# Attention with a gated MLP mixer on one core: score tiles in two 2-bank and three 1-bank PSUM buffers, half of the 64-shifts on GpSimd, conversions ahead of shifts, and a new first and last step

## The chip, the cores and the metric

The kernel runs on one core of one Trainium2 chip. The metric is the device time of one execution in microseconds (us), smaller is better. A core has these engines: TensorE (PE in the profile; PEld is its weight load), VectorE (DVE), ScalarE (ACT), GpSimd (POOL) and SyncE (SP, which here only issues DMAs). SBUF is the on-chip memory; PSUM, of which this kernel fills eight banks of 128 x 512 fp32 (seven for scores and projections, one for the accumulator), is where TensorE leaves its results.

## The reference, cut to what matters

```python
# x: 1 x 2048 x 512, 32 heads of 16 dimensions
g = sigmoid((x * gate_w).sum(-1, keepdims=True))
qkv = (x @ wqkv) ...                       # q, k, v by heads
scores = einsum("bhqd,bhkd->bhqk", q, k) * (16 ** -0.5)
a = einsum("bhqk,bhkd->bhqd", softmax(scores), v) ... @ wo
b = <layernorm, w1, gelu, shifts along S, w2, residual, layernorm, w3, gelu, w4, residual>
return g * a + (1 - g) * b
```

The costly part is the softmax: 32 heads x 2048 x 2048 scores are 2048 tiles of 128 x 512 exponentials.

## The kernel before

The tiles are worked off in 32 rounds of 64. TensorE computes transposed scores into PSUM. Each tile's exponential is then done by one of two engines.

ScalarE takes groups of three or two tiles at a time with one `activation`:

```python
WIDTHS, RING = (3, 2), 2          # psA buffers of 3 and 2 banks for ScalarE; 2 single banks for the rest
NPA, NPD, NW = 6, 16, 9
...
job = act(hold, ops, lambda: nc.scalar.activation(out=pb.slot[:, 0:n], in_=buf.slot[:, 0:n], func=ACT.Exp,
                                                  scale=0.25), acq=[pb], frees=[buf], prio=3)
```

VectorE builds its exponentials out of bits. A conversion ("p1") turns a score tile from a single PSUM bank into uint16 numbers that, read as bf16, are a rough exponential. For each pair of tiles these numbers are then shifted by 32, 64 and 96, and all four patterns are multiplied by V, so that their average is a good exponential. A VectorE tile therefore costs TensorE four P·V matmuls where a ScalarE tile costs one. The shifts by 32 and 64 are VectorE's, the third is GpSimd's:

```python
        def p1():
            nc.vector.tensor_scalar(out=pr["buf"].slot[:, h * 512:(h + 1) * 512], in0=buf.slot[:], scalar1=BITS_MUL,
                                    scalar2=BITS_ADD, op0=ALU.mult, op1=ALU.add)
        j1 = dve(598, [o], p1, acq=[pr["buf"]] if h == 0 else [], frees=[buf], prio=2, name="p1")
    # ... cut ...
        for k in range(1, 4):
            def sh(k=k):
                d = [b.slot for b in bufs]
                if k < 3:
                    nc.vector.tensor_scalar(out=d[k][:, 0:w], in0=d[0][:, 0:w], scalar1=float(SHIFT * k), scalar2=None,
                                            op0=ALU.add)
                else:
                    nc.gpsimd.tensor_scalar(out=d[k][:, 0:w], in0=d[2][:, 0:w], scalar1=1.0, scalar2=float(SHIFT),
                                            op0=ALU.mult, op1=ALU.add)
            if k < 3:
                j = dve(0.26 * w + 72.0, pr["jobs"], sh, prio=1, acq=[bufs[k]], frees=[bufs[0]])
            else:
                j = gp(0.833 * w + 165.0, last, sh, prio=1, acq=[bufs[k]], frees=[bufs[2]])
```

Which tile goes to which engine, and in what order each engine issues its instructions, is fixed when the program is built. The kernel has its own planner, a small event model of the engines (`class Sim`): the first number in `act(...)`, `dve(...)` and `gp(...)` is how long the planner believes the instruction holds its engine in ns, and the ready job with the lowest `prio` goes first. A pair's shift, 1024 elements wide, is planned at 0.26 x 1024 + 72 = 338 ns on VectorE and 0.833 x 1024 + 165 = 1018 ns on GpSimd. **The planner treats the engines as independent.**

At the end of each round the accumulator is copied, its denominators are gathered, inverted and spread by DMAs, GpSimd multiplies (`oT`), and DMAs pack the product into `oD` buffers for the output projection.

The softmax here doesn't subtract the row's maximum and nothing guards it: scores larger than these inputs give would overflow.

Of the kernel before, what the change touches and what calls it, by code (L numbers as in the profile page):

```python
# [75 lines left out]
class Gen:  # L76


    def __init__(self, units, deps, at, name, acq="ring"):
        self.units, self.deps, self.at, self.name = units, deps, at, name  # L80
        self.pos = 0
        self.buf = Buf(acq, 1)
        self.ops = [o for u in units for o in u]
        self.gone = False
# [144 lines left out]
def kernel(  # L229
# [27 lines left out]
    WIDTHS, RING = (3, 2), 2  # L257

    NPA, NPD, NW = 6, 16, 9
# [8 lines left out]
    def slots(name, n, shape, dt=BF16, where=const):  # L268
# [10 lines left out]
    zero = const.tile([P, 512], BF16, name="zero")  # L279
    mE = const.tile([P, 1], F32, name="mE")  # L280
# [18 lines left out]

    sim = Sim({  # L300
        **{f"psA{w}{n}": slots(f"psA{n}", 1, [P, 512 * w], F32, ps) for n, w in enumerate(WIDTHS)},
        "ring": slots("ring", RING, [P, 512], F32, ps),
        "PA": slots("PA", NPA, [P, 1536]),
# [50 lines left out]
    for c0, c1 in ((0, 128), (128, 512)):  # L354
        nc.scalar.dma_start(out=W("k")[:, :, c0:c1], in_=wrows(A_wqkv[:, D + c0:D + c1]))
        nc.scalar.dma_start(out=wq[:, :, c0:c1], in_=wrows(A_wqkv[:, c0:c1]))
    nc.scalar.dma_start(out=W("v")[:], in_=wrows(A_wqkv[:, 2 * D:3 * D]))
    nc.scalar.dma_start(out=gw[:], in_=gate_w.rearrange("(kt p) -> p kt", p=P))
    dl_w["k0"] = sim.add(Job("SP", 1, 6000.0, [], None))
    dl_w["k"] = sim.add(Job("SP", 1, 12000.0, [], None))  # L360
    dl_w["v"] = sim.add(Job("SP", 1, 14000.0, [], None))
# [6 lines left out]
    for c in range(NCH):  # L368
        for k in range(KT):
            j_xT[c, 0, k] = load_xT(c, k, 0, 2600.0 + 1150.0 * (4 * c + k + 1), 0)  # L370
    for c in range(NCH):
        j_x.append(dma(22000.0 + 2000.0 * c, [], lambda c=c: nc.sync.dma_start(
            out=x_sb[:, 4 * c:4 * c + 4, :], in_=x_flat[c * 512:(c + 1) * 512, :].rearrange("(t p) d -> p t d", p=P)),
            prio=1))
# [13 lines left out]

    gp(150, [], lambda: nc.gpsimd.memset(mhalf[:], -0.5), prio=0)
    j_io = gp(200, [], lambda: nc.gpsimd.iota(mi[:], pattern=[[0, 1]], base=0, channel_multiplier=1), prio=0)  # L390
    j_z = dve(300, [], lambda: nc.vector.memset(zero[:], 0.0), prio=0)
    j_m1 = dve(100, [j_io], lambda: nc.vector.tensor_scalar(out=mb[:], in0=mi[:], scalar1=16, scalar2=None,
# [11 lines left out]
    def gen(name, at, deps, mms, N=512, M=P):  # L404

        get = lambda: g.buf.slot
        units = []
        for i, (lf, rf) in enumerate(mms):
            st, sp = i == 0, i == len(mms) - 1
            if COL and M == P:  # L410
                units.append([Op("col", j, lambda j=j, lf=lf, rf=rf, st=st, sp=sp: nc.tensor.matmul(  # L411
                    get()[32 * j:32 * j + 32, 0:N], lhsT=lf(32 * j, 32 * j + 32), rhs=rf(), start=st, stop=sp,
                    tile_position=(0, 32 * j), skip_group_check=True), ns=N * 0.42, name=name) for j in range(4)])
            else:
                units.append([Op("full", None, lambda lf=lf, rf=rf, st=st, sp=sp: nc.tensor.matmul(
                    get()[0:M, 0:N], lhsT=lf(0, M), rhs=rf(), start=st, stop=sp), ns=N * 0.42, name=name)])
        g = Gen(units, deps, at, name)
        gens.append(g)
        return g
# [8 lines left out]

    j_k = {}

    def k_proj(G, c, at):
# [3 lines left out]
        g.ops[-1].frees += [wb["k"], wb[f"x{c}0"]]  # L435
        j_k[G, c] = evac(g, PSUM_NS, lambda ps: nc.vector.tensor_copy(out=kT[G][:, c * 512:(c + 1) * 512], in_=ps[:]),
# [5 lines left out]
    def q_proj(G, c, at):  # L442
# [3 lines left out]
                  lambda k=k: W(f"x{c}{part}")[:, k, :]) for k in range(KT)])  # L446
# [21 lines left out]
    def v_proj(t, at):  # L468
        c = t // 4
        g = gen("v", at, [j_xT[c, 0, k] for k in range(KT)] + [dl_w["v"]],  # L470
                [(lambda a, b, k=k: W(f"x{c}0")[:, k, (t % 4) * P + a:(t % 4) * P + b],
                  lambda k=k: W("v")[:, k, :]) for k in range(KT)])
        g.ops[-1].frees += [wb["v"], wb[f"x{c}0"]]
        j_v[t] = evac(g, PSUM_NS, lambda ps: nc.vector.tensor_copy(
            out=V0[:, t, :, 1:DH + 1], in_=ps[:].rearrange("p (h d) -> p h d", h=H)), prio=2)
        j_v[t].deps.append(j_v1)
        if t % 2 == 0:
            j_v2[t] = gp(750, [j_v[t]], lambda: nc.gpsimd.tensor_scalar(
                out=V2[:, t // 2], in0=V0[:, t], scalar1=W2, scalar2=1.0, op0=ALU.mult, op1=ALU.mult), prio=1)


    def gate(at):
        g = gen("z", at, [j_xT[c, 0, k] for c in range(NCH) for k in range(KT)], [], M=P)
# [97 lines left out]
    j_o2 = {}  # L581

    def mlp2(c, s2, at_of, jgate):
        last = normalise(c, 1, [s2[t] for t in range(4 * c, 4 * c + 4)], 0)
        jx1g = {}
        for t in range(4 * c, 4 * c + 4):
# [15 lines left out]
        for t in range(4 * c, 4 * c + 4):  # L602
# [13 lines left out]
            else:  # L616
                j_o2[t] = evac(g, PSUM_NS, lambda ps, t=t: nc.vector.scalar_tensor_tensor(
                    out=x_sb[:, t, :], in0=ps[:], scalar=omg[:, t:t + 1], in1=x_sb[:, t, :], op0=ALU.mult,
                    op1=ALU.add))
                sim.jobs["DVE"][-1].deps.append(jx1g[t])  # L620

    def mix(g, t, deps):
        ob = Buf("ot", 1)
# [265 lines left out]
    for t in range(NT):  # L889
        v_proj(t, max(0, 3 * t - 2))  # L890
# [197 lines left out]
```

## Time and profile before

Three executions took 891.75 to 893.7 us, median 893.31.

| | before |
|---|---|
| median time | 893.3 us |
| tiles done by ScalarE / by VectorE | 1534 / 514 |
| ScalarE busy in the long stretches | 94% |
| first exponential starts | 12.6 us |
| longest wait of ScalarE in mid run | 14.6 us |
| last exponential ends, to the end | 24 us |

First the page of the kernel before: busy time of each engine with its share of the span, three of the rows that show the span in 40 slices (each digit is a busy share in tenths), and the chain of work that ended last, by engine.

```profile
PE 786.6 (89%) x8981; PEld 251.1 (28%) x8982; DVE 693.1 (78%) x1361; ACT 755.7 (85%) x631; POOL 390.5 (44%) x400
...
DVE  4774988798899998877875787678878568887871
ACT  3364999899998999998993998999998889999990
POOL 2243764444467793434432444234444234344440
...
PE 48%; ACT 23%; DVE 12%; issue 7%; DMA 4%; POOL 4%; SPq 2%; POOLq 0%; ACTq 0%; DVEq 0%
```

After the first four slices ScalarE sits at 8s and 9s, with a dip to 3 in slice 22; VectorE and GpSimd have room. The chain runs mostly through PE and ScalarE.

Next the same page's costliest groups: line, engine, operation, output from input, shapes and count; then total busy us and mean ns of one; then the engine's idle time before them and who ended most of it.

```profile
L741 ACT ACTIVATE PA<-psA 128x1536 bf16<-128x1536 f32 x614 | 709.7, 1259 | 97.8 <-PE acc L821 38.4
L793 POOL TENSOR_SCALAR PD<-PD 128x1024 uint16<-128x1024 uint16 x257 | 269.8, 1050 | 432.4 <-DVE PD L790 310.4
L766 DVE TENSOR_SCALAR PD<-ring 128x512 uint16<-128x512 f32 x514 | 340.7, 682 | 106.6 <-PE ring L665 90.1
...
L790 DVE TENSOR_SCALAR PD<-PD 128x1024 uint16<-128x1024 uint16 x514 | 219.5, 464 | 6.3 <-PE acc L821 0.7
```

The four kinds of work in question: exponentials (L741), GpSimd's shift (L793), VectorE's conversions from PSUM (L766) and VectorE's shifts (L790). The shifts' mean of 464 ns hides a wide spread, as all the instructions of that one line show (minimum, median, maximum in ns):

```profile
L790 DVE TENSOR_SCALAR PD<-PD x514: 359/419/1501, 14.1 to 861.8; 128x1024 uint16<-128x1024 uint16 x172
```

Half of the shifts take 419 ns or less.

Last, the windows view of the kernel before: start and end of the stretch, its length, and busy us of PE, PEld, DVE, ACT and POOL (instructions in brackets), then TensorE's clock, DMA share and GB/s.

```profile
0.00:100.00 100.00, 79.14 (x858) 25.68 (x858) 64.26 (x133) 53.14 (x47) 38.80 (x52) 0.91 0.41 97
100.00:470.00 370.00, 332.22 (x3751) 105.20 (x3754) 319.79 (x632) 346.21 (x292) 192.83 (x196) 0.97 0.17 45
470.00:490.00 20.00, 16.16 (x239) 6.38 (x235) 10.16 (x18) 4.99 (x6) 6.00 (x6) 1.00 0.09 28
490.00:865.00 375.00, 352.51 (x4134) 111.82 (x4123) 294.72 (x574) 351.35 (x291) 151.60 (x147) 0.95 0.08 22
865.00:889.00 24.00, 6.62 (x16) 2.04 (x16) 4.12 (x7) 0.00 (x0) 1.26 (x1) 0.63 0.12 37
```

ScalarE is busy 346.21 of 370 us and 351.35 of 375, 94% in both. The other three rows are the head, a stall and the tail.

### The profile page before, as it was taken

The page shows a single profiled execution, that of the slowest core. Times are in us where ns is not written, and L with a number is a line of the kernel's source. Part 1 is how long each engine was busy: PE and PEld are TensorE (multiplying, and loading weights), DVE is VectorE, ACT ScalarE, POOL GpSimd, SP SyncE. Part 2 cuts the span into 40 slices and gives each one's busy share as a digit, 9 for nine tenths or more (in the row PEclk, how much of TensorE's full clock was granted, in tenths as well). Part 3 has the DMA queues.
Part 4 walks back from the last instruction along what each step waited for, and adds up shares of the span by engine and source line. Part 5 has one row for each costly group of instructions (what it writes and reads, how often), then busy time and mean ns, then how long its engine had stood idle before and what let it go on. Part 6 is the DMA issues. An engine that isn't in the chain of part 4 may idle for free.

```text
span 888.9 us, 22112 instructions
## 1 busy us (share of the span) xinstructions
PE 786.6 (89%) x8981; PEld 251.1 (28%) x8982; DVE 693.1 (78%) x1361; ACT 755.7 (85%) x631; POOL 390.5 (44%) x400
## 2 busy tenths in 40 slices
PE   5996899898898989979898998999988999989982
PEld 1331233322222223322233332333312333323220
DVE  4774988798899998877875787678878568887871
ACT  3364999899998999998993998999998889999990
POOL 2243764444467793434432444234444234344440
PEclk9987999999799999988999996999978999979996
DMA  8512211103013140011000001001000100000001
GB/s 165 168 31 39 82 51 23 38 24 117 17 45 76 46 124 6 18 42 32 14 20 26 24 18 41 26 24 35 18 16 17 30 27 17 14 7 18 18 17 39
DMA packets 71302, 35.83 MB, mean 40 GB/s; under 512 B 51360, under 2 KB 66464, under 8 KB 71200
## 3 DMA queue, kind: packets, MB, share of 16 engines
q1 hardware_dynamic: 68032, 32.84, 14.1%
q10 hardware_dynamic: 3168, 1.57, 0.8%
q8 instruction: 70, 1.15, 0.5%
q14 instruction: 32, 0.26, 0.1%
HBM read 17.60 MB, written 6.82 MB: 27 GB/s over the span
## 4 chain that ended last, share of the span: by engine, by line
PE 48%; ACT 23%; DVE 12%; issue 7%; DMA 4%; POOL 4%; SPq 2%; POOLq 0%; ACTq 0%; DVEq 0%
ACT PA L741 18%; PE acc L821 17%; PE ring L411 17%; PE psA L665 11%; DVE PD L766 5%; DVE PD L790 3%; ACT hT L600 3%; PE ring L665 3%; POOL PD L793 2%; DMA zE_dram<-zE 1%; DVE st L509 1%; POOL xn L529 1%; SPq L364 1%; ACT hT L567 1%; DMA w<-in_A_x_dram 1%
## 5 line engine op out<-in xcount | busy, mean ns | idle before, releaser
L741 ACT ACTIVATE PA<-psA 128x1536 bf16<-128x1536 f32 x614 | 709.7, 1259 | 97.8 <-PE acc L821 38.4
L793 POOL TENSOR_SCALAR PD<-PD 128x1024 uint16<-128x1024 uint16 x257 | 269.8, 1050 | 432.4 <-DVE PD L790 310.4
L766 DVE TENSOR_SCALAR PD<-ring 128x512 uint16<-128x512 f32 x514 | 340.7, 682 | 106.6 <-PE ring L665 90.1
L821 PE MATMUL acc<-PD,V 128*17 128x512 bf16 x2056 | 328.8, 401 | 25.4 <-DVE PD L790 10.5
L821 PE MATMUL acc<-PA,V 128*17 128x512 bf16 x1534 | 292.7, 389 | 2.8 <-DVE accsb L834 2.0
L665 PE MATMUL psA<-q,kT 32*128 32x512 bf16 x1534 | 240.6, 395 | 35.4 <-ACT PA L741 33.5
L790 DVE TENSOR_SCALAR PD<-PD 128x1024 uint16<-128x1024 uint16 x514 | 219.5, 464 | 6.3 <-PE acc L821 0.7
L665 PE MATMUL ring<-q,kT 32*128 32x512 bf16 x514 | 179.1, 402 | 6.1 <-DVE PD L766 5.6
L821 PEld LDWEIGHTS <-V 128*17 128x17 bf16 x3590 | 95.6, 89 | 222.3 <-issue 176.5
L665 PEld LDWEIGHTS <-kT 32*128 32x128 bf16 x2048 | 74.2, 91 | 277.0 <-issue 272.5
L411 PE MATMUL ring<-xnT,w 128*32 128x512 bf16 x1152 | 82.6, 381 | 4.2 <-DVE PD L766 1.3
L411 PE MATMUL ring<-w,hT 128*32 128x512 bf16 x1152 | 84.0, 387 | 1.5 <-DVE x_sb L576 0.8
L411 PEld LDWEIGHTS <-w 128*32 128x32 bf16 x1664 | 45.2, 98 | 56.4 <-issue 32.9
L851 POOL TENSOR_TENSOR oT<-accsb,bcs 128x512 bf16<-128x512 f32 x32 | 41.1, 1283 | 25.1 <-DMA bcs<-rr 18.7
L598 DVE CAST hT<-ring 128x512 bf16<-128x512 f32 x56 | 38.4, 685 | 9.7 <-PE ring L411 9.2
L411 PE MATMUL ring<-w,w 128*32 128x512 bf16 x512 | 44.5, 430 | 1.6 <-DVE PD L766 0.8
L411 PEld LDWEIGHTS <-hT 128*32 128x32 bf16 x1152 | 30.2, 97 | 36.7 <-issue 18.4
L529 POOL TENSOR_SCALAR xn<-x_sb,rs,nm 128x512 bf16<-128x512 bf16 x32 | 29.6, 934 | 1.9 <-DVE nm L522 1.6
L411 PE MATMUL ring<-w,wq 128*32 128x512 bf16 x256 | 20.8, 395 | 8.1 <-DMA w<-in_A_x_dram 6.9
L834 DVE COPY accsb<-acc 128x512 f32<-128x512 f32 x32 | 21.8, 682 | 6.0 <-PE acc L821 5.8
L600 ACT ACTIVATE hT<-hT 128x7168 bf16<-128x7168 bf16 x4 | 24.7, 6177 | 0.0
L509 DVE BATCH_NORM_STATS2 st<-x_sb 128x6 f32<-128x512 bf16 x32 | 21.7, 679 | 0.1
(49 smaller groups left out, 213.4 us busy)
## 6 DMA issues: line engine op xcount, KB each, us to landing
bcs<-rr SPq DMA_DIRECT2D x128, 64.0 KB
xn_dram<-xn SPq DMA_DIRECT2D x32, 128.0 KB
w<-in_B_w_dram SPq DMA_DIRECT2D x5, 512.0 KB
x_sb<-in_A_x_dram SPq DMA_DIRECT2D x4, 512.0 KB
oD<-oT SPq DMA_DIRECT2D x128, 16.0 KB
out_dram<-ot SPq DMA_DIRECT2D x16, 128.0 KB
w<-in_B_w_dram SPq DMA_DIRECT2D x4, 448.0 KB
w<-in_A_wqkv_dram ACTq DMA_DIRECT2D x1, 512.0 KB
```

What stands on the lines that cost most here:

```text
L411: units.append([Op("col", j, lambda j=j, lf=lf, rf=rf, st=st, sp=sp: nc.tensor.matmul(get()[32 * j:32 * j + 32, 0:N], lhsT=lf(32 * j, 32 * ...
L509: a = dve(600, deps, lambda: nc.vector.bn_stats(out=sb.slot[:], in_=x_sb[:, t, :]), prio=6, at=at, acq=[sb])
L529: g = gp(760, [m], lambda t=t, xb=xb: nc.gpsimd.tensor_scalar(out=xb.slot[:], in0=x_sb[:, t, :], scalar1=rs[which][:, t:t + 1], scalar2=nm ...
L598: pre.append(evac(g, PSUM_NS, lambda ps, m=m: nc.vector.tensor_copy(out=h2[:, m, :], in_=ps[:]), acq=[bb] if m == 0 else []))
L600: ge = act(93 + 427 * FT + 2600, pre, lambda: nc.scalar.activation(out=h2, in_=h2, func=ACT.Gelu_apprx_tanh), prio=0)
L665: o = Op("row", i, lambda: nc.tensor.matmul(dst(), lhsT=kT[G][32 * i:32 * i + 32, kt * P:(kt + 1) * P], rhs=qbuf[G, c].slot[32 * i:32 * i ...
L741: job = act(hold, ops, lambda: nc.scalar.activation(out=pb.slot[:, 0:n], in_=buf.slot[:, 0:n], func=ACT.Exp, scale=0.25), acq=[pb], frees= ...
L766: nc.vector.tensor_scalar(out=pr["buf"].slot[:, h * 512:(h + 1) * 512], in0=buf.slot[:], scalar1=BITS_MUL, scalar2=BITS_ADD, op0=ALU.mult, ...
L790: nc.vector.tensor_scalar(out=d[k][:, 0:w], in0=d[0][:, 0:w], scalar1=float(SHIFT * k), scalar2=None, op0=ALU.add)
L793: nc.gpsimd.tensor_scalar(out=d[k][:, 0:w], in0=d[2][:, 0:w], scalar1=1.0, scalar2=float(SHIFT), op0=ALU.mult, op1=ALU.add)
L821: o = Op("col", i, lambda: nc.tensor.matmul(acc[32 * i:32 * i + DH + 1, :], lhsT=lhs(), rhs=rhs(), start=st, stop=True, tile_position=(0, ...
L851: n = gp(1250, d3, lambda: nc.gpsimd.tensor_tensor(out=ob.slot[:], in0=ab.slot[:], in1=bb.slot[:], op=ALU.mult), acq=[ob], frees=[ab, bb], ...
```

## The change

Its intent is to shorten head and tail, to have a third single bank so that more tiles can go to VectorE, to take a quarter of VectorE's shift work away, and to keep ScalarE fed. The core of the diff, with cuts marked and comments added:

```diff
-    WIDTHS, RING = (3, 2), 2
-    NPA, NPD, NW = 6, 16, 9
+    WIDTHS, RING = (2, 2), 3
+    NPA, NPD, NW = 9, 16, 9
+    P1_PRIO = 0.5                 # conversions now go before shifts (prio 1); they went after them (2)
+    GP2 = 0.5                     # every second pair gives its 64-shift to GpSimd
...
-        j1 = dve(598, [o], p1, acq=[pr["buf"]] if h == 0 else [], frees=[buf], prio=2, name="p1")
+        j1 = dve(598, [o], p1, acq=[pr["buf"], pr["token"]] if h == 0 else [], frees=[buf], prio=P1_PRIO, name="p1")
...
     def close_pair(pr):
+        evs["n"] = evs.get("n", 0.0) + GP2
+        both = evs["n"] >= 1.0
+        if both:
+            evs["n"] -= 1.0
...
-                if k < 3:
+                if k == 1 or k == 2 and not both:
                     nc.vector.tensor_scalar(out=d[k][:, 0:w], in0=d[0][:, 0:w], scalar1=float(SHIFT * k), scalar2=None,
                                             op0=ALU.add)
                 else:
-                    nc.gpsimd.tensor_scalar(out=d[k][:, 0:w], in0=d[2][:, 0:w], scalar1=1.0, scalar2=float(SHIFT),
-                                            op0=ALU.mult, op1=ALU.add)
+                    nc.gpsimd.tensor_scalar(out=d[k][:, 0:w], in0=d[0 if both else 2][:, 0:w], scalar1=1.0,
+                                            scalar2=float(SHIFT * (k if both else 1)), op0=ALU.mult, op1=ALU.add)
...
+    x_transposes(0)               # first chunk of x transposed by TensorE, copied out by ScalarE and VectorE
+    x_transposes(1)
...
+            j_xT[0, 0, k] = (dve if k % 2 else act)(500, g.units[-1], cp, prio=0, frees=[g.buf])
...
-            q_proj(G, c, 128 * r0 - 50)
+            q_proj(G, c, 128 * r0 - QAT)          # QAT = 110; generators now chosen by when they are due
...
+    lasts = [last_gen(tt) for tt in range(3)]     # three of the last four output banks prepared ahead
...                                # last round: denominators inverted and spread by TensorE instead of by DMAs
```

The planner's numbers for an instruction's hold are as before. Not shown: `token`, which lets five pairs be under way at once, V projections in two halves, the warm-up of ScalarE and TensorE, and the limits that name the planner's old constants.

## The prediction

> **What bounds the kernel now.** Busy time by stretch of the 888.9 us span: from 0 to 100 us ScalarE is busy 53; from 100 to 470, 346 of 370 (94%), PE 332, VectorE 320; from 470 to 490, ScalarE 5; from 490 to 865, 351 of 375 (94%), PE 353, VectorE 295; from 865 to 889 it does nothing. The long stretches are bound by ScalarE's exponentials, PE close behind; the rest is head, stall and tail.
>
> **Tail.** In the timeline the last exponential ends near 865; then come the accumulator's copy, five DMA hops until 879.8, 16 matmuls at half clock (5.5 us) and the stores: 24 us. The change leaves no DMA before the store and prepares three of four output banks early. Estimate from durations here (copies 0.4, small matmuls 1.5, reciprocal 0.4, broadcast and product 1.5, projection and eviction 1.5, store 3): 9 us. Gain 15.
>
> **Stall at 475 to 490.** ScalarE's longest wait (14.6 us). PE ran w3/w4 generators one by one through the ring, each waiting for its eviction, while the next query projection came only at 486.5. The change orders generators by due count, issues query projections 60 tiles earlier and has three ring buffers. Gain 13.
>
> **Head.** First exponential now at 12.6 us, behind transposing DMAs and projections; about 8.5 with the first chunk transposed on PE. Half the V projections can wait, with nine probability buffers for six; ScalarE's waits for accumulating matmuls in the first 100 us are 22 us. VectorE's stall from 70 to 78 us, behind the 11 us zE store, should stay. Gain 12.
>
> **Middle.** Exponentials of 1024 columns take 1047 ns, of 1536 1472, but fifteen back to back took 17.39 us, 0.46 per tile; I estimate 0.467 for two-wide ones, +13 us over 1484 tiles. Against that, VectorE's two shifts per pair (mean 464 ns) become one and a half, 60 us less for 257 pairs; GpSimd gains 135. The third ring buffer should let VectorE take about 50 more tiles (564 for 514), 23 us less on ScalarE. But each such tile costs PE four PV matmuls instead of one, and PE alternates row and column tiling more often (742 exponentials for 614). The Trainium skill's "TensorEngine Tiling (Array Packing)", Key Properties, says that a change of tiling mode drains the array; the trace shows gaps of 0.2 to 0.4 us in weight loads there. Its "SBUF — State Buffer", Who interferes with whom, says that a VectorE two-port operation and a GpSimd one block each other; here a shift took 359 to 1501 ns, which agrees with waiting out a 1044 ns GpSimd shift. Net gain 3.
>
> **Sum.** 893.3 - 15 - 13 - 12 - 3 = 850 us, range 824 to 877. Chances: faster by over 2% 0.90, within 2% 0.08, slower 0.02.
>
> **Right or wrong in the profile.** Tail: under 12 us after the last exponential. Stall: no wait of ScalarE over 8 us between 100 and 860. Head: ScalarE busy 62 us or more in the first 100. Middle: ScalarE 92 to 96% busy; 540 to 600 VectorE tiles; mean VectorE shift longer than 464 ns; PE at 90% or more.
>
> **What would make it wrong.** PE becoming the limit through mode changes, ScalarE below 90% in the middle; VectorE blocked by GpSimd, taking no more tiles; the new fixed order meeting a DMA later than planned and stalling all engines; or VectorE taking 100 more tiles, 25 us more gained.

## The result, and the profile after

The changed kernel gives a correct result and takes 950.35 us (948.46 to 950.73, four executions), against 893.5 for the kernel before in the same rounds. The ratio is 1.0634 (95% interval 1.0612 to 1.0656). Ratios in this text are the mean time of one kernel's fast runs over that of the other's fast runs of the same rounds, so they are not quite the ratio of the medians that stand beside them. The change made the kernel 6.3% slower where a gain of 5% was predicted.

| | before | predicted | after |
|---|---|---|---|
| median time, us | 893.5 | 850 | 950.35 |
| VectorE tiles | 514 | 564 | 671 |
| VectorE busy, us | 693.1 | – | 858.3 |
| mean VectorE shift, ns | 464 | above 464 | 657 |
| ScalarE busy from 100 to 470 us | 94% | 92–96% | 81% |
| first exponential, us | 12.6 | 8.5 | 21.4 |
| longest mid-run wait of ScalarE, us | 14.6 | under 8 | 13.1 |
| from the last exponential's end, us | 24 | 9 | 17 |

The page of the kernel after, the same lines as shown of before:

```profile
PE 838.4 (88%) x9869; PEld 258.6 (27%) x9869; DVE 858.3 (90%) x1509; ACT 720.2 (76%) x713; POOL 669.6 (71%) x655
...
DVE  2988999998999999998995899899899998999993
ACT  2875778878988769787774778887688676899882
POOL 1676878877768878997764676677578676677772
...
DVE 56%; PE 26%; issue 7%; DMA 5%; SPq 3%; POOL 2%; ACT 1%; ACTq 0%; DVEq 0%; POOLq 0%
```

VectorE is now at 8s and 9s throughout, ScalarE at 7s and 8s, and the chain that ended last runs 56% through VectorE, where it was 12%. The limit has moved from ScalarE to VectorE. Now the same groups:

```profile
L842 ACT ACTIVATE PA<-psA 128x1024 bf16<-128x1024 f32 x689 | 670.7, 1022 | 194.8 <-PE ring L765 116.6
L899 POOL TENSOR_SCALAR PD<-PD 128x1024 uint16<-128x1024 uint16 x504 | 550.8, 1110 | 202.7 <-DVE PD L896 69.6
L867 DVE TENSOR_SCALAR PD<-ring 128x512 uint16<-128x512 f32 x671 | 438.6, 675 | 24.3 <-PE ring L765 20.7
...
L896 DVE TENSOR_SCALAR PD<-PD 128x1024 uint16<-128x1024 uint16 x504 | 322.0, 657 | 2.9 <-PE acc L930 0.4
```

L842 is the old L741, L899 the old L793, L867 the old L766, L896 the old L790. Two things grew on VectorE: 671 conversions for 514, +97.9 us, and the shifts, which are fewer (504 for 514) but take 322.0 us for 219.5. Together +200 us; the rest of VectorE's work shrank by 35, so it is busy 165 us longer. The change was to make the shifts cheaper. Per VectorE tile they cost 219.5 / 514 = 427 ns before and 322.0 / 671 = 480 ns after: with a quarter of them given away, the shifts cost VectorE more per tile, not less.

(Count x mean is 3 to 9% more than the page's sum in these groups, since the records of neighbouring instructions overlap a little and the page counts the overlap once. In this text the sums are the page's, and the means are used for single instructions.)

The instructions of L896 alone (minimum, median, maximum in ns):

```profile
L896 DVE TENSOR_SCALAR PD<-PD x504: 278/429/1498, 23.9 to 930.4; 128x1024 uint16<-128x1024 uint16 x168
```

The median is still 429 ns. The mean rose to 657 through the long ones. What do long ones look like? This is the timeline of the kernel after around 300 us, VectorE and GpSimd: start, duration, engine, line.

```profile
299.19 2.22 POOL L899 TENSOR_SCALAR PD<-PD 128x1024 uint16<-128x1024 uint16 x2
299.44 1.07 DVE L896 TENSOR_SCALAR PD<-PD 128x1024 uint16<-128x1024 uint16 x1
...
300.52 1.17 DVE L896 TENSOR_SCALAR PD<-PD 128x1024 uint16<-128x1024 uint16 x1
```

GpSimd runs two shifts back to back from 299.19 (its row is the two together); in the single records behind the row the first ends at 300.23 and the second at 301.41. VectorE's first shift starts at 299.44 and ends at 300.51; its second starts at 300.52 and ends at 301.69. Each ends 0.28 us after a GpSimd shift does: it stood still until GpSimd's instruction was over and then ran. I counted this over whole traces ("in flight": a GpSimd instruction had begun before the shift did and went on for over 20 ns more):

```
VectorE shifts: count, mean ns | GpSimd in flight at the start: count, mean | else: mean | sum of time above 400 ns, us
before           514, 464      |  90, 680                                   | 418        |  33
after            504, 657      | 325, 792                                   | 411        | 130
```

Shifts that start while GpSimd is idle take 411 to 418 ns in both kernels. What changed is the share that meets GpSimd: 18% before, 64% after. Of the shifts that took 700 ns or more, the middle 80% end 278 to 284 ns after a GpSimd instruction ends, in both kernels (median 280). The conversions, which read PSUM, were never lengthened: mean 675 to 683 ns, with 99% of them under about 693.

The Trainium skill, "SBUF — State Buffer", section "Who interferes with whom", describes this: GpSimd uses the second pair of VectorE's SBUF ports, a VectorE operation in a two-port mode needs both pairs, and whichever issues first has the shared pair for its whole instruction while the other waits. It lists `tensor_scalar` among the operations that can do so, and operations with at most one SBUF input outside those modes among those that do not. The trace agrees on both counts, with the numbers above; in which mode an operation ran, a trace does not show.

The windows of the kernel after (columns as before):

```profile
100.00:470.00 370.00, 326.60 (x3619) 95.91 (x3616) 359.32 (x644) 300.82 (x297) 295.37 (x291) 0.95 0.17 45
...
500.00:526.00 26.00, 21.92 (x351) 9.17 (x354) 12.87 (x23) 9.27 (x11) 9.09 (x10) 1.00 0.10 29
526.00:930.00 404.00, 368.86 (x4315) 107.31 (x4308) 380.82 (x650) 326.45 (x318) 285.80 (x263) 0.96 0.08 20
930.00:949.00 19.00, 13.99 (x174) 6.84 (x173) 3.68 (x10) 2.84 (x5) 2.22 (x3) 0.89 0.09 29
```

From 100 to 470 us VectorE is busy 359.32 of 370 us (97%) and ScalarE 300.82 (81%, it was 94%). There is still a stall, now at 500 to 526, and a tail of 19.

The head, in the timeline of ScalarE of each kernel. Before:

```profile
11.27 1.28 ACT L741 ACT_TABLE_LOAD   x1 [11.27 <-DMA wq<-in_A_wqkv_dram]
12.56 2.37 ACT L741 ACTIVATE PA<-psA 128x1536 bf16<-128x1536 f32 x2
```

After (ACTq is ScalarE's sequencer issuing a DMA):

```profile
14.40 0.42 ACTq L402 DMA_DIRECT2D gw<-in_gate_w_dram  x1
14.85 1.28 ACT L448 ACT_TABLE_LOAD   x1 [14.85 <-DMA w<-in_A_x_dram]
...
16.26 1.05 ACT L502 COPY w<-ring 128x512 bf16<-128x512 bf16 x2
20.18 0.59 ACT L514 CAST kT<-ring 128x512 bf16<-128x512 f32 x1 [2.87 <-PE ring L474]
21.37 4.69 ACT L842 ACTIVATE PA<-psA 128x1024 bf16<-128x1024 f32 x5 [0.60 <-PE psA L765]
```

ScalarE issues eight loads first. The last issue is at 14.40 us; only then does it load its table, and copy the transposed chunk (L502) at 16.26, although TensorE's transposes were over by 6.4 us. TensorE waits for that copy:

```profile
4.58 1.75 PE L493 MATMUL ring<-idb,x_sb 128*128 128x128 bf16 x16
16.88 1.93 PE L474 MATMUL ring<-w,wq 128*32 128x512 bf16 x16 [10.55 <-ACT w L502]
```

The tail after, in the timeline:

```profile
931.33 0.60 ACT L842 ACTIVATE PA<-psA 128x512 bf16<-128x512 f32 x1 [0.83 <-PE psA L765]
...
932.90 1.06 PE L474 MATMUL ring<-w,idf 128*32 128x512 f32 x1
...
937.97 1.43 PE L474 MATMUL ring<-wo,oD 128*32 128x512 bf16 x16
...
939.33 1.05 PE L1177 MATMUL psA<-idf,accsb 128*128 128x4 f32 x8
```

The last exponential is over at 931.93. The denominators' matmul (L1177) could follow the accumulator's copy, which ended at 934.82, but TensorE first works through the "prepared" banks (L474) from 932.90 until 939.33. They were not ready early; they run at the worst time. Of their 6.4 us, the last 4.5, after the copy, delay the denominators.

### The profile page after: what moved, and what is told of

It reads as the page before. It is cut to its first block, busy times and chain, and to the rows that moved or that the text cites. A ratio compares the mean times of both kernels' runs of the same rounds, so it can differ in the third digit from the quotient of the medians.

```text
span 948.9 us, 24548 instructions
## 1 busy us (share of the span) xinstructions
PE 838.4 (88%) x9869; PEld 258.6 (27%) x9869; DVE 858.3 (90%) x1509; ACT 720.2 (76%) x713; POOL 669.6 (71%) x655
## 4 chain that ended last, share of the span: by engine, by line
DVE 56%; PE 26%; issue 7%; DMA 5%; SPq 3%; POOL 2%; ACT 1%; ACTq 0%; DVEq 0%; POOLq 0%
DVE PD L867 26%; DVE PD L896 21%; PE ring L474 10%; PE acc L930 8%; PE psA L765 6%; DVE hT L681 2%; SPq L409 2%; DVE accsb L946 1%; DMA pk<-den 1%; DVE st L594 1%; DMA zE_dram<-zE 1%; POOL PD L899 1%; PE ring L765 1%; DVE pk L954 1%; DVE hT L650 1%
## 5 line engine op out<-in xcount | busy, mean ns | idle before, releaser
L842 ACT ACTIVATE PA<-psA 128x1024 bf16<-128x1024 f32 x689 | 670.7, 1022 | 194.8 <-PE ring L765 116.6
L899 POOL TENSOR_SCALAR PD<-PD 128x1024 uint16<-128x1024 uint16 x504 | 550.8, 1110 | 202.7 <-DVE PD L896 69.6
L867 DVE TENSOR_SCALAR PD<-ring 128x512 uint16<-128x512 f32 x671 | 438.6, 675 | 24.3 <-PE ring L765 20.7
L930 PE MATMUL acc<-PD,V 128*17 128x512 bf16 x2684 | 363.0, 402 | 49.9 <-DVE PD L896 26.8
L896 DVE TENSOR_SCALAR PD<-PD 128x1024 uint16<-128x1024 uint16 x504 | 322.0, 657 | 2.9 <-PE acc L930 0.4
L765 PE MATMUL psA<-q,kT 32*128 32x512 bf16 x1377 | 262.5, 396 | 7.3 <-ACT PA L842 6.4
L765 PE MATMUL ring<-q,kT 32*128 32x512 bf16 x671 | 225.4, 399 | 21.6 <-DVE PD L867 19.7
L765 PEld LDWEIGHTS <-kT 32*128 32x128 bf16 x2048 | 65.7, 91 | 262.1 <-issue 259.9
L474 PE MATMUL ring<-xnT,w 128*32 128x512 bf16 x1152 | 82.7, 387 | 10.5 <-DVE PD L867 6.5
L474 PE MATMUL ring<-w,hT 128*32 128x512 bf16 x1152 | 85.8, 391 | 2.9 <-DVE PD L867 1.5
L474 PEld LDWEIGHTS <-w 128*32 128x32 bf16 x1920 | 48.4, 97 | 67.8 <-issue 49.6
L963 POOL TENSOR_TENSOR oT<-accsb,bcs 128x512 bf16<-128x512 f32 x31 | 41.0, 1321 | 21.2 <-DMA oD<-oT 14.6
L474 PEld LDWEIGHTS <-hT 128*32 128x32 bf16 x1152 | 28.7, 97 | 44.9 <-issue 30.0
L474 PE MATMUL ring<-w,w 128*32 128x256 bf16 (+1 forms) x768 | 38.5, 319 | 1.1 <-DVE PD L867 0.8
L474 PE MATMUL ring<-w,wq 128*32 128x512 bf16 x256 | 20.1, 421 | 10.7 <-ACT w L502 10.6
L562 POOL TENSOR_SCALAR V<-V 128x272 bf16<-128x272 bf16 x16 | 7.1, 441 | 23.2 <-DVE V L557 22.1
```

The source lines that it names most:

```text
L474: units.append([Op("col", j, lambda j=j, lf=lf, rf=rf, n0=n0, n1=n1, st=st, sp=sp: nc.tensor.matmul(get()[32 * j:32 * j + 32, n0:n1], lhsT ...
L765: o = Op("row", i, lambda: nc.tensor.matmul(dst(), lhsT=kT[G][32 * i:32 * i + 32, kt * P:(kt + 1) * P], rhs=qbuf[G, c].slot[32 * i:32 * i ...
L899: nc.gpsimd.tensor_scalar(out=d[k][:, 0:w], in0=d[0 if both else 2][:, 0:w], scalar1=1.0, scalar2=float(SHIFT * (k if both else 1)), op0=A ...
L930: o = Op("col", i, lambda: nc.tensor.matmul(acc[32 * i:32 * i + DH + 1, :], lhsT=lhs(), rhs=rhs(), start=st, stop=True, tile_position=(0, ...
L963: n = gp(1250, d3, lambda: nc.gpsimd.tensor_tensor(out=ob.slot[:], in0=ab.slot[:], in1=bb.slot[:], op=ALU.mult), acq=[ob], frees=[ab, bb], ...
```

## The experiments

### The theory and its rivals

- Theory A, exclusion: VectorE's shifts wait for GpSimd's instructions, more often than before because there are more of those and because the new order puts shifts next to them; the planner does not know it and loads VectorE beyond what it can do.
- Rival B, amount: VectorE was simply given too many tiles (671), and would be too slow without any waiting.
- Rival C, GpSimd's latency: GpSimd itself (71% busy) finishes its shifted patterns late, so TensorE waits and buffers stay taken.
- Rival D, layout: narrower exponentials and more mode changes on TensorE cost the time.

Kernels with "after" in the edit are built from the changed kernel, those with "before" from the old one. All 18 passed the comparison with the reference, also the two that are wrong; for those two the comparison was evidently too coarse to tell.

### short_gp: GpSimd's shifts made short

Edit to after; wrong, since only 64 of 1024 columns are shifted. The order of instructions on every engine is the same as in the changed kernel, but for 16 clearing instructions at the start, without which the program would read memory that nobody has written.

```diff
-  nc.gpsimd.tensor_scalar(out=d[k][:, 0:w], in0=d[0 if both else 2][:, 0:w], scalar1=1.0,
+  nc.gpsimd.tensor_scalar(out=d[k][:, 0:64], in0=d[0 if both else 2][:, 0:64], scalar1=1.0,
+ (16 memsets of the PD buffers on GpSimd at the start)
```

> The changed kernel with the same order on every engine; only each GpSimd shift works on 64 columns in place of 1024 (16 memsets at the start make the buffers defined). Wrong output on purpose. Lock theory (VectorE shifts wait out GpSimd shifts): mean VectorE shift falls from 657 to about 420 ns, VectorE busy falls by about 110 us, and the time falls from 950 to about 850 us. Rival (too many tiles on VectorE, or PE with four matmuls per VectorE tile, is the limit by itself): shift time may fall, but the time stays above 910 us.

Measured: 852.85 us, ratio to before 0.9558 (0.9517 to 0.96), 97 us less than the changed kernel. The group of VectorE's shifts in this run:

```profile
L896 DVE TENSOR_SCALAR PD<-PD 128x1024 uint16<-128x1024 uint16 x504 | 212.7, 441 | 2.9 <-PE acc L930 0.2
```

The mean shift fell from 657 to 441 ns. The same 671 tiles now take VectorE 742.8 us, so rival B is out as the whole story: the amount is bearable without the waits. Rival C is not yet out, since GpSimd was quicker too.

### reduce_dve: GpSimd in full, VectorE's shift replaced by something that does not take the shared ports

Edit to after; wrong. VectorE's shift becomes a `tensor_reduce` of 256 columns, of about the length of an undisturbed shift. The Trainium skill, same page and section, says of `tensor_reduce` that on trn2 it never contends.

```diff
-  nc.vector.tensor_scalar(out=d[k][:, 0:w], in0=d[0][:, 0:w], scalar1=float(SHIFT * k), scalar2=None, op0=ALU.add)
+  nc.vector.tensor_reduce(out=d[k][:, 0:1], in_=d[0][:, 0:256], axis=mybir.AxisListType.X, op=ALU.max)
+ (16 memsets of the PD buffers on GpSimd at the start)
```

> The changed kernel, order unchanged, GpSimd shifts at full size (1024 columns); in place of each VectorE shift a VectorE reduction of 256 columns to one, about as long as an unblocked shift, an operation that should not use the shared port pair. Wrong output on purpose. Lock theory: the reductions take about the same time whether or not a GpSimd shift is in flight (spread under 100 ns), VectorE busy about 110 us less, time 845 to 870 us, although GpSimd is as busy as in the changed kernel. Rival (what helped in short_gp was that GpSimd's results came earlier, not that VectorE stopped waiting): time stays above 920 us.

Measured: 849.84 us, 0.9516 (0.9482 to 0.9549). All instructions of that line (minimum, median, maximum):

```profile
L896 DVE TENSOR_REDUCE PD<-PD x504: 358/409/422, 25.2 to 831.2; 128x1 uint16<-128x256 uint16 x168
```

From 358 to 422 ns: no instruction was lengthened, although 373 of the 504 began with a GpSimd instruction in flight, and GpSimd was busy 639.9 us. This agrees with the page. It also puts rival C out: GpSimd did all of its work (its own shifts took 1043 ns on average, 1110 in the changed kernel) and the kernel is still 100 us faster. What costs those 100 us is VectorE standing still for GpSimd. The two runs together show theory A's cause; neither is a usable kernel.

### gp2_zero: only the 64-shift put back to VectorE

```diff
-    GP2 = 0.5
+    GP2 = 0.0
```

> The changed kernel with no 64-shift on GpSimd (as before the change), planned anew: 646 VectorE tiles for 671. Lock theory alone: the mean shift returns to about 464 ns as before, but there are about 646 shifts for 504, so VectorE stays the limit: its busy time is about 840 us and the time 910 to 940 us. If moving half of the 64-shifts were the whole cause: under 870 us.

Measured: 996.7 us, 1.1168 (1.1118 to 1.1218); 646 VectorE tiles. This was a clear miss: I had expected 910 to 940, from a mean shift of 464 ns as before. Fewer GpSimd instructions are not enough:

```profile
L896 DVE TENSOR_SCALAR PD<-PD 128x1024 uint16<-128x1024 uint16 x646 | 358.2, 583 | 2.8 <-issue 0.9
```

The mean is 583 ns, and 273 of 646 shifts started with GpSimd in flight (before: 90 of 514), with about the same GpSimd shifts per tile as before. So something else in the change puts the shifts behind GpSimd. The obvious candidate is the order, conversions first.

### order_back and order_back_gp2_zero: the old order of conversions and shifts

Edits to after:

```diff
-    P1_PRIO = 0.5
+    P1_PRIO = 2
```

and, for the second, also `GP2 = 0.0`.

> The changed kernel with VectorE's old priorities: the shifts of a pair go before the next pair's conversion from the score buffer (the change had put the conversions first); half of the 64-shifts still on GpSimd; 646 VectorE tiles. Order theory (a shift that is put off until GpSimd has begun the pair before's shift waits for it): the mean shift falls from 657 to 560 to 620 ns and the time from 950 to 905 to 935 us. If the order does not matter: within 10 us of 950.

> The changed kernel with the old priorities and no 64-shift on GpSimd; 626 VectorE tiles. It differs from gp2_zero (996 us, mean shift 583 ns) in the order of VectorE's work alone. Order theory: mean shift 460 to 500 ns as in before_psum (475), time 865 to 890 us. If gp2_zero was slow for another reason, such as its queue order: above 930 us.

Measured: order_back 916.98 us, 1.0269 (1.023 to 1.0308), mean shift 610 ns, 646 tiles. order_back_gp2_zero 886.59 us, 0.9914 (0.9888 to 0.9939), mean shift 483 ns, 626 tiles. Both times fell in the range expected of the order theory. The shifts of order_back_gp2_zero, to be held against those of gp2_zero above:

```profile
L896 DVE TENSOR_SCALAR PD<-PD 128x1024 uint16<-128x1024 uint16 x626 | 279.0, 483 | 6.4 <-PE acc L930 2.4
```

The changed kernel's two settings thus form a square (medians in us):

| | 64-shifts half on GpSimd | all on VectorE |
|---|---|---|
| conversions first | 950 | 997 |
| shifts first, as before | 917 | 887 |

With the old order, moving 64-shifts to GpSimd costs 30 us; with the new order it saves 46. The order, with the plan made anew for it (25 or 20 VectorE tiles fewer), costs 33 or 110 us. The traces of the right column show what it does, conversions and shifts matched in the order of pairs. With shifts first, a pair's first shift starts 0.52 us after its second conversion ends (median; mean 0.61) and the second follows at once. With conversions first it starts 1.88 us after (mean 3.04), and the second another 0.52 us later; the second of a pair then meets a GpSimd instruction in flight in 109 of 323 pairs, for 61 of 313. How much of the 110 us is such waiting, and how much is that the shifted patterns come later for everybody else, no run separates.

### before_gp2_half, before_psum, before_psum_gp2: parts of the change alone, in the old kernel

Edits to before: the first takes over `GP2 = 0.5` and the code that goes with it; the second the PSUM layout alone; the third both.

```diff
 (before_psum)
-    WIDTHS, RING = (3, 2), 2
-    NPA, NPD, NW = 6, 16, 9
+    WIDTHS, RING = (2, 2), 3
+    NPA, NPD, NW = 9, 16, 9
...
-        "PA": slots("PA", NPA, [P, 1536]),
+        "PA": slots("PA", NPA, [P, 1024]),
```

> The kernel before with one part of the change alone: of every second pair the 64-shift goes to GpSimd as well; 521 VectorE tiles for 514. Lock theory: the mean VectorE shift rises from 464 to above 600 ns, but there are only 390 shifts for 514, so VectorE is at most 40 us busier and not yet the limit: 885 to 915 us. Rival (the part is harmless or useful by itself): 860 to 885 us.

> The kernel before with another part alone: two 2-bank buffers and three shared 1-bank buffers (and nine buffers for probabilities); 638 VectorE tiles for 514, all 64-shifts on VectorE. If the third shared buffer hurts by letting the planner load VectorE beyond what it can do: VectorE busy above 93% of 100 to 850 us and the time 925 to 965 us. Rival (the layout is good and only the GpSimd part hurts): below 880 us.

> The kernel before with both parts, buffers and half of the 64-shifts, without the change's head, tail and queue order; 669 VectorE tiles. If these two parts explain the loss: 940 to 970 us, near the changed kernel's 950. If the head, tail or queue order carry the loss: below 920 us.

Measured:

| | median us | ratio | 95% | VectorE tiles | mean shift ns |
|---|---|---|---|---|---|
| before | 893.1 | | | 514 | 464 |
| before_gp2_half | 901.93 | 1.0088 | 1.0064–1.0112 | 521 | 560 |
| before_psum | 887.39 | 0.9931 | 0.991–0.9952 | 638 | 475 |
| before_psum_gp2 | 935.14 | 1.0462 | 1.0436–1.0487 | 669 | 611 |

The layout by itself, with the plan that it allows, is worth 6 us, so rival D does not explain the loss; what the narrower exponentials cost before VectorE's extra tiles make up for it is not separated. GpSimd's extra shifts by themselves cost 9. Together they cost 42, far more than the sum: the layout lets the planner hand VectorE some 125 to 150 tiles more, and the lengthened shifts then fall on an engine that is busy 90% of the span (842.8 of 934.9 us). This interaction needs none of the other parts, and 42 us is most of the change's loss of 57. The expectations were met in part: before_psum is neither above 925 nor below 880, the shifts of before_gp2_half stayed under 600 ns, and before_psum_gp2 came out 5 us under its range.

### cap17 and gp2_zero_cap17: fewer tiles for VectorE, a confounded try

Edit to after, `DVE_CAP = 99` to 17 tiles per round; for the second also `GP2 = 0.0`.

> The changed kernel with at most 17 VectorE tiles in a round of 64 (541 tiles for 671), half of the 64-shifts still on GpSimd. If the number of VectorE tiles is what hurts: ScalarE is the limit again, 860 to 885 us, although the shifts still wait for GpSimd (mean 600 ns or more). If the waits alone hurt whatever the number: above 910 us.

> Both: no 64-shift on GpSimd and at most 17 VectorE tiles in a round (542). Mean shift about 464 ns, VectorE busy about 740 us. With both causes gone, and head and tail of the change kept: 865 to 885 us. If it is not below cap17, then moving half of the 64-shifts costs nothing at this number of tiles.

Measured: 966.2 us, 1.0835 (1.079 to 1.0879), with 541 tiles; and 948.72, 1.0656 (1.0597 to 1.0715), with 542. In cap17 neither VectorE (75%) nor ScalarE (80%) is near its limit. The cap counts from the start of a round, so VectorE gets its 17 tiles at once and none at the end of the round: from 240 to 250 us of cap17 it is busy 0.06 us. The two engines stop running side by side. The granted clock was lower too, 0.907 to 0.928 in these runs against 0.944 to 0.951 in the changed kernel. By its expectation cap17 speaks for the waits alone, and gp2_zero_cap17 missed its range by over 60 us; I take neither as evidence about the amount, and made another cut.

### even572 and even510: fewer tiles, spread over the round

Edit to after, with 19 (even572) and 17 (even510) in place of N:

```diff
-  if n_left(r) <= DVE_STOP or sum(n_dve[r]) >= DVE_CAP:
+  if n_left(r) <= DVE_STOP or 64 * sum(n_dve[r]) > N * (64 - n_left(r)) + 64:
```

> As even510 with 572 tiles. Overload theory: between even510 and the changed kernel, 890 to 925 us. Waits alone: above 930 us.

> The changed kernel, half of the 64-shifts on GpSimd and conversions first as in it, but VectorE's tiles held, evenly through each round, to 510 in all (671 in it, 514 before). If overloading VectorE is what turns the waits into lost time: VectorE busy below 80% and 885 to 910 us, although the mean shift stays at 600 ns or more. If the waits delay the other engines whatever VectorE's load: above 930 us, as cap17 (966).

Measured: even572 904.67 us, 1.0142 (1.0107 to 1.0177), 572 tiles, mean shift 596 ns, VectorE 82% busy. even510 914.94 us (median of its three fast runs), 1.0249 (1.0185 to 1.0312); its profiled run, slow (clock 0.917), is not compared. Taking 99 tiles from VectorE gives 46 us back, so the amount matters, given the waits. even510 lies between its two expectations, and even572 lies under it where it was expected above. Even with the load taken off, both are slower than the kernel before. That the waits cost without overload too is likely, but these runs don't isolate it, since the changed kernel's late head and order are in them as well. Why 510 tiles are slower than 572 I did not find out; the granted clock of even510's fast runs was 0.920 to 0.939, that of even572's 0.942 to 0.948.

### order_gp2_head: ScalarE out of the head's way

Edit to after: as order_back_gp2_zero, and the copies of the transposed chunk and of the first keys go to VectorE, whose sequencer issues no DMAs in this kernel.

```diff
-            j_xT[0, 0, k] = (dve if k % 2 else act)(500, g.units[-1], cp, prio=0, frees=[g.buf])
+            j_xT[0, 0, k] = dve(500, g.units[-1], cp, prio=0, frees=[g.buf])
 (and the same for the copy into kT)
```

> As order_back_gp2_zero, and in the head the copies of the transposed first chunk and the first key copy are on VectorE in place of ScalarE, whose sequencer is held by its own DMA issues until 14.4 us. If that held the head back: first exponential near 12 us in place of 21, and 6 to 10 us less than order_back_gp2_zero. If the weights' DMAs are what is late: the same within 3 us.

Measured: 877.28 us, 0.9818 (0.9785 to 0.9852), 9 us less than order_back_gp2_zero. TensorE's and ScalarE's timelines of this run:

```profile
6.21 1.17 PE L474 MATMUL ring<-w,wq 128*32 128x512 bf16 x16 [0.29 <-DMA wq<-in_A_wqkv_dram]
...
11.17 0.40 PE L765 MATMUL psA<-q,kT 32*128 32x512 bf16 x4
```

```profile
15.90 0.39 ACTq L402 DMA_DIRECT2D gw<-in_gate_w_dram  x1
...
17.72 3.75 ACT L842 ACTIVATE PA<-psA 128x1024 bf16<-128x1024 f32 x4
```

The first scores come at 11.17 us (22.0 in order_back_gp2_zero), so the copy on ScalarE was what held TensorE. The first exponential comes at 17.72 (22.45 there), not near 12 as expected, since ScalarE still issues its eight loads, the last at 15.90. That is the next thing to move; no run did it.

### lock_order: a planner that knows the exclusion

Edit to after: `GP2 = 0.0`, the head of order_gp2_head, conversions first, and in the planner a VectorE shift and a GpSimd instruction may not overlap; shifts go as soon as GpSimd is free.

```diff
+        if e == "POOL" and self.two_until > self.t:
+            return False
...
+            if j.two and self.t_free["POOL"] > self.t:
+                continue
```

> No 64-shift on GpSimd, the head as in order_gp2_head, conversions first as in the change, but the planner knows the exclusion: a VectorE shift starts only when GpSimd is idle, GpSimd only when no VectorE shift runs, and shifts come first once GpSimd is idle; 624 VectorE tiles. If the plan's order is followed on the chip: mean shift below 450 ns and 845 to 875 us. If the chip's times stray too far from the plan's for the order to help: mean shift above 500 ns, above 890 us.

Measured: 890.0 us, 0.9947 (0.9914 to 0.998), mean shift 492 ns. A miss: it is slower than order_gp2_head (877), which uses the plain old order. 48 shifts still took 1000 ns or more. The plan is a fixed order of instructions, not a clock, and on the chip GpSimd and VectorE drift apart from the planned times; that this drift is why it failed is argued, not shown.

### balance556 and balance588: is the split right now?

Edit: order_gp2_head with the even limit at 18 and at 21.

> order_gp2_head (no 64-shift on GpSimd, shifts before conversions, head copies on VectorE; 877 us with 626 tiles) with VectorE's tiles held evenly to 556. If VectorE was still the limit there: 860 to 875 us. If it was balanced already: 878 to 895, ScalarE the limit again.

> As balance556 with 588 tiles. If VectorE was still the limit at 626: 862 to 874 us. If balanced already: 875 to 885 us.

Measured: 880.52 us, 0.9873 (0.9848 to 0.9898), with 556 tiles; 878.35, 0.985 (0.9825 to 0.9874), with 588; order_gp2_head has 877.28 with 626. The three ratios lie within 0.6% of each other: with the waits this small (mean shift 475 to 488 ns), the number of tiles hardly matters between 556 and 626.

### before_od7 and best_od7: one more buffer for finished rounds

ScalarE's waits on accumulating matmuls in the two kernels (line, what it waited for, total us, times and longest); the longest is the stall:

```profile
ACT PA L741 <- PE acc L821: 38.4, 14, 14.6
```

```profile
ACT PA L842 <- PE acc L930: 25.5, 13, 13.1
```

In the stall, GpSimd waits to multiply a finished round because the packing DMAs of an earlier one have not gone out. The timeline of GpSimd in the stall of the kernel before, and then of the kernel after:

```profile
486.38 1.27 POOL L851 TENSOR_TENSOR oT<-accsb,bcs 128x512 bf16<-128x512 f32 x1 [6.43 <-DMA oD<-oT]
```

```profile
521.91 1.27 POOL L963 TENSOR_TENSOR oT<-accsb,bcs 128x512 bf16<-128x512 f32 x1 [11.87 <-DMA oD<-oT]
```

The DMA that it waits for needs a free `oD` buffer, and these buffers come free when the last output-projection matmuls that read them are done. In the kernel after, these run from 516.15, the packing DMAs are issued from 516.59, GpSimd multiplies at 521.91, the accumulating matmuls go on at 524.49 and the exponentials at 525.83. Edit: seven instead of six, in the kernel before (before_od7), and in order_gp2_head (best_od7, where one xn buffer is given up for the room; eight did not fit in memory).

```diff
-slots("oD", 6, [P, 512])
+slots("oD", 7, [P, 512])
 (best_od7 also)
-slots("xn", 4, [P, D])
+slots("xn", 3, [P, D])
```

> The kernel before with seven buffers for finished rounds in place of six, planned anew (507 VectorE tiles for 514). If these buffers make the stall: no wait of ScalarE over 6 us between 100 and 860 us, and 878 to 887 us. If late queries make it: the wait of 14 us stays and the time stays at 890 to 895.

> order_gp2_head with seven buffers for finished rounds, and three for normalised rows in place of four to make room (616 VectorE tiles for 626). Buffers make the stall: its wait of 17.5 us goes, and 862 to 872 us for 877. Otherwise 875 to 882.

Measured: best_od7 872.18 us (870.01 to 873.41), 0.9739 (0.969 to 0.9788): 2.6% faster than the kernel before, and the fastest correct kernel. ScalarE's waits on accumulating matmuls as above; first order_gp2_head, then best_od7:

```profile
ACT PA L842 <- PE acc L930: 23.2, 6, 17.5
```

```profile
ACT PA L842 <- PE acc L930: 20.1, 18, 4.9
```

The single wait of 17.5 us is gone; the longest is now 4.9. The plan was made anew (616 tiles for 626), so the buffer is not quite isolated, and the time is at the edge of what was expected. In the kernel before the same buffer gives 0.9909 (0.9848 to 0.997); one of its four runs, the profiled one, was slow (1045.83 us, clock 0.642) and is left out, so its profile can't show where its gain lies. The three fast runs (883.1, 886.52 and 890.92) reach from one expectation into the other.

## Why the prediction was wrong

| step of the prediction | predicted | measured |
|---|---|---|
| tail | −15 | −7 |
| stall | −13 | −1.5 |
| head, by ScalarE's busy time in the first 100 us | −12 | −7 |
| middle (what is left) | −3 | about +72 |
| sum | −43 | +57 |

- **The step that failed: "VectorE's two shifts per pair (mean 464 ns) become one and a half, 60 us less for 257 pairs".** It multiplied the mean of before by the new count. That mean was no constant: it was 418 ns for an undisturbed shift, plus waiting for GpSimd. The same change nearly doubled GpSimd's shift time (269.8 to 550.8 us) and moved shifts behind conversions. At that price a VectorE tile costs 1.5 x 464 / 2 = 348 ns of shifts; it cost 504 x 657 / 671 = 493, more than the 464 of before. The time above 400 ns each rose from 33 to 130 us in all. The prediction named the exclusion, the very place in the skill and the sign of it ("mean VectorE shift longer than 464 ns"), but gave it no size, and so the sum counted it as nothing. short_gp and reduce_dve, with the order and the share of work of the changed kernel, put its size at 97 and 100 us of kernel time. The moved shifts are not its only source: gp2_zero moves none and still has a mean of 583 ns, through the order.
- **"VectorE should take about 50 more tiles", and "ScalarE 92 to 96% busy".** The planner gave it 157 more. Its own sum, which is no measurement, has VectorE busy 717.6 us for the changed kernel; the trace shows 858.3. It plans 338 ns for a shift that took 657. (It is low in the kernel before too, 627.8 for 693.1, as it also plans 598 ns for a conversion that takes 682; the gap grew from 65 to 141 us.) So ScalarE fell to 81% and VectorE became the limit. "VectorE taking 100 more tiles" stood under what would make the prediction wrong, but as a gain of 25 us; it was a loss.
- **"VectorE blocked by GpSimd, taking no more tiles"** was right in its first half only. A plan fixed at build time does not react: a blocked engine is given its tiles all the same. Where the layout let the planner give it more, the cost of 9 us (before_gp2_half) became 42 (before_psum_gp2).
- **Order.** The prediction did not name the new priority of conversions at all. order_back shows that it costs 33 us in the changed kernel, and gp2_zero against order_back_gp2_zero 110, each with its own plan.
- **Head.** The first exponential came at 21.4 us, not at 8.5: copies of the transposed chunk, for which the first projections wait, were put on the engine whose sequencer was held by eight DMA issues until 14.4 us. The Trainium skill, "DMA: Bandwidth & Descriptors", section "Issuing engines are not separate DMA queues", calls the sequencer's time to start a DMA usually small relative to the DMA itself; here one issue is 0.4 to 0.5 us, but the queue of eight, with up to 4.5 us from the start of one to the start of the next, held ScalarE for 14 us; what the gaps wait for no run shows. Later in the first 100 us the gain came anyway: ScalarE was busy 60.0 us for 53.1, against 62 or more predicted.
- **Stall.** The prediction blamed generators going through the ring one by one, and late query projections. The stall stayed at 13.1 us with the generators reordered, the queries earlier and three ring buffers, and a wait of 17.5 us went when a seventh `oD` buffer was added to order_gp2_head. The path from the generators to ScalarE was wrong: it ran over the `oD` buffers. That those buffers come free late because the generators run one by one is still true in the trace.
- **Tail.** 17 us, not 9: right in mechanism (no DMA is left before the store), wrong in that the prepared banks held up the denominators for 4.5 us. Without these it would still be 12.5 us by subtraction, as the other steps were underestimated too. No run tried to prepare the banks earlier, so that its gain is 4.5 us is only argued.
- **PE at 90% or more** was wrong for the changed kernel (88%); it is 92% in the two runs without the waits, where ScalarE is at 83 and 84%. So although those runs take about the predicted 850 us, that is luck: they do not confirm the prediction's picture of a kernel bound by ScalarE.

Still open: why even510 is slower than even572; what the waits cost at a load that VectorE can bear; why the planner that knows the exclusion does no better; what the stalls of gp2_zero (one wait of ScalarE of 34.0 us) come from; and how much of best_od7's remaining 872 us the tail and ScalarE's loads would give.

## What to carry to other kernels

Before you move work from VectorE to GpSimd, split the duration of the VectorE operation by whether a GpSimd instruction was in flight at its start; if the two differ (here 418 and 680 ns), the mean is not a price, and the work moved may cost more than it frees. Where a planner fixes the order and the share of work, compare its busy sums with the trace's before trusting what it does with a new degree of freedom, for an unmodelled wait comes back as a wrong split. And put nothing that the first matmuls wait for on an engine whose sequencer is still issuing DMAs.

## What the Trainium skill lacked or had wrong

- "SBUF — State Buffer", section "Who interferes with whom": right in every point that the runs touched (`tensor_scalar` SBUF to SBUF blocked, conversions from PSUM and `tensor_reduce` not). It names two slowdowns, measured in opposite issue orders, but no cost for a mix of instructions. Here a 128 x 1024 uint16 shift of 411 ns took 792 on average when a GpSimd instruction of about 1.05 us was in flight at its start, and shifts of 700 ns or more ended 280 ns after that instruction did.
- The same section tells who blocks, but not that the order within VectorE's own queue decides how often it happens. Here putting conversions before shifts raised the mean shift from 483 to 583 ns with GpSimd's work per tile unchanged (order_back_gp2_zero and gp2_zero).
- "DMA: Bandwidth & Descriptors", section "Issuing engines are not separate DMA queues": it calls the time to start a DMA usually small. The section does not say that several DMAs issued in a row by an engine that also computes can hold its sequencer far longer than the 0.4 to 0.5 us that each issue shows: here eight issues on ScalarE held it until 14.4 us, and moving two kinds of copies from it to VectorE brought the first scores from 22.0 to 11.2 us.
- "TensorEngine Tiling (Array Packing)", Key Properties, on the drain at a change of tiling mode, which the prediction used: no run here measured it by itself. before_psum, with 722 ScalarE instructions for 631, was no slower.
